# Residual vector quantiser on one core: four shared double PSUM tiles, score tiles of eight groups, another rule for idle products, and a new plan

## The chip, the core and the metric

The kernel runs on one core of a Trainium2 chip. A core has five engines that run side by side, each with an instruction queue of its own: PE (TensorE, matrix products, which write PSUM), DVE (VectorE), ACT (ScalarE), POOL (GpSimd) and SP (SyncE, which here only issues DMAs). PSUM has eight banks; in this kernel a bank holds 512 f32 per partition. The metric is device time in microseconds for one launch; lower is better. One profiled execution, with a trace, stands beside the timed runs.

## What is computed

Input x is (2, 16000, 512) in bf16. A three-tap convolution over time, one weight per tap and channel, is followed by SiLU. Four stages of a residual quantiser follow: in each, the nearest of eight code words is found for every token, subtracted from the residual and added to q. A second three-tap convolution of q gives the output.

```python
for i in range(K):
    z = z + xp[:, i:i+T, :] * dw_enc[i][None, None, :]
z = _silu(z)
for s in range(Nq):                       # Nq = 4, 8 code words each
    d2 = |res|^2 - 2 res.cb + |cb|^2      # (B, T, 8)
    sel = cb[d2.argmin(-1)]
    q = q + sel;  res = res - sel
y = three-tap convolution of q with dw_dec
```

## The kernel before

**Tiling.** The 32,000 tokens form 250 groups of 128, and token p*250+g sits in group g, so the neighbour in time of a token is in the next group at the same place. The groups are worked on in 16 chunks of 12, 14 times 16, and 14 groups (`SIZES`, L26). Channels lie on the 128 partitions in four blocks of 128 (`KT`).

**Front of a chunk** (`front`, L496). SP loads x transposed (L458), up to four groups a DMA. For each channel block DVE makes three tap products (L523). Their two additions run on DVE (L531) or as accumulating DMAs that POOL issues (L529). SiLU is exp, +1, log, exp (ACT L535, DVE L539, ACT L543, L546) and a product on DVE (L551) that writes the residual tile RES. The first chunk is loaded in rows instead (L272, L275), transposed on PE (L427) and copied out of PSUM, blocks 0 and 2 by ACT (L434) and 1 and 3 by DVE (L432).

**A stage** (`stage`, L584). RES holds, beside each 64 tokens, the code words. One product of those 64 tokens with themselves and the code words (L612) therefore gives each token's norm on a diagonal and its products with the eight words. Another product adds a large negative number off the diagonal (L606, `MASK`). DVE takes the maximum of each row, which is the norm (L620), and copies the eight products (L623). A score tile takes up to `GB` = 6 groups, so a chunk of 16 groups has three of 6, 5 and 5. Five small DVE steps (L642 to L666) turn all 16 groups into a one-hot code, PE transposes it (L676), DVE copies it to OHT (L683). In the first three stages RES is then renewed in eight pieces of 1024 elements for two halves of the groups and four channel blocks: either PE forms the selected words (SEL, L700) and DVE adds them (L716), or PE adds words to the old residual (NEW, L721 and L700) and ACT writes it back (L727). After the last stage PE forms the output (Y, L753), ACT copies it (L759) and SP stores it (L763).

**PSUM.** Pool `psG` has two tiles of one bank, for score tiles alone; pool `psA` has three tiles of two banks, for SEL, NEW, Y, the transposed one-hots and the setup (L222, L223).

**Who sets the order.** All steps are tasks of a planner (`Plan`, L55): engine, time held, delay, needs, due time, and the slots that it takes and gives back. A pass puts every task on its engine as soon as engine, needs and slots are free, by rank; passes run forward and backward from ranks with random noise (`ROUNDS`, L47: seed, noise, number of passes). The plan's order is emitted as it stands and every engine runs its own in sequence. A DMA is modelled on one of the servers "SP" (transposing loads), "ACC" (accumulating DMAs) and "OUT" (stores), each with its own line of work.

**Idle products.** Where the plan leaves PE a gap of at least 0.3 us, a psG tile is free and PE was planned busy for less than 60% of the last 4 us, `emit` (L159) puts products into the gap that nobody reads (`warm`, L398; they go to the next score tile, which overwrites them). `ahead` (L409) runs 40 more near the start.

## Time and profile before

| | us |
|---|---|
| three timed runs | 739.68, 749.41, 775.06 (median 749.41) |
| the profiled execution's own time | 744.72 |
| its span, first to last instruction | 742.9 |
| DVE busy in the span | 687.8 |
| ACT busy in the span | 666.7 |
| PE busy in the span | 597.4 |
| mean granted TensorE clock | 0.926 of full speed |

The busy time of an engine counts each moment once. The granted clock is the share of full speed that TensorE was given; a matrix product takes twice as long where it is 0.50. A row such as `L620 DVE TENSOR_REDUCE TR<-PS` names the line of the kernel, the engine, the operation and what is written from what. The duration of one instruction can be longer than the distance to the next one on the same engine, because the next one starts while the last one still ends.

### The profile page before, as it was taken

What the parts mean: (1) busy time and instruction counts of PE and PEld (TensorE: products, weight loads), DVE (VectorE), ACT (ScalarE), POOL (GpSimd) and SP (SyncE); (2) the same over time, 40 slices, a digit from 0 to 9 for tenths busy, and PEclk for the clock granted to TensorE, in tenths of its full rate; (3) what the DMA queues carried; (4) which work ended last, traced back from release to release, by engine and by line L of the source; (5) the groups of instructions that cost most, each with busy time, mean ns of one, the idle gap of its engine ahead of it and who ended that gap; (6) DMA issues with size and microseconds to landing.
All of it is one profiled execution on the core that took longest, in us unless ns stands there. A gap on an engine that the chain in (4) does not pass through costs nothing.

```text
span 742.9 us, 23573 instructions
## 1 busy us (share of the span) xinstructions
PE 597.4 (80%) x10485; PEld 314.9 (42%) x10552; DVE 687.8 (93%) x1359; ACT 666.7 (90%) x539; POOL 78.3 (11%) x104
## 2 busy tenths in 40 slices
PE   4047677898889897888889888988788889889986
PEld 4033334453444344444435443544444443454542
DVE  6999999998999999999999999999999999899942
ACT  2779879998999999999999998989999999975686
POOL 3022100100100011010101001010110001000000
PEclk9558899998998899999999998999999998899999
DMA  7899975979494779668794787979995426220235
GB/s 174 136 188 188 189 136 103 149 137 199 115 209 92 154 175 215 113 175 183 185 210 120 132 164 182 126 210 131 213 185 141 118 58 175 55 88 2 88 142 227
DMA packets 160832, 111.14 MB, mean 150 GB/s; under 512 B 142425, under 2 KB 142810, under 8 KB 160602
## 3 DMA queue, kind: packets, MB, share of 16 engines
q1 hardware_dynamic: 148976, 69.61, 40.2%
q0 software_dynamic: 11472, 39.76, 29.2%
q8 instruction: 82, 1.34, 0.8%
q10 hardware_dynamic: 282, 0.26, 0.1%
q14 instruction: 20, 0.16, 0.1%
HBM read 2.39 MB, written 32.77 MB: 47 GB/s over the span
## 4 chain that ended last, share of the span: by engine, by line
ACT 42%; DVE 28%; PE 17%; issue 5%; DMA 5%; SPq 1%; ACTq 0%; DVEq 0%
ACT RES L727 14%; ACT YSB L759 8%; ACT LN L543 8%; DVE RES L716 8%; ACT E L535 7%; ACT E L546 5%; PE NEW L721 4%; DVE TR L620 3%; PE PS L612 3%; DVE RES L551 3%; PE Y L753 3%; DVE T L523 3%; PE NEW L700 2%; DVE Z L531 2%; DVE E L539 2%
## 5 line engine op out<-in xcount | busy, mean ns | idle before, releaser
L727 ACT ACTIVATE RES<-NEW 128x1024 bf16<-128x1024 f32 (+1 forms) x218 | 219.5, 1052 | 28.4 <-PE NEW L700 21.4
L716 DVE TENSOR_TENSOR RES<-RES,SEL 128x1024 bf16<-128x1024 bf16 (+1 forms) x166 | 196.8, 1197 | 4.1 <-PE SEL L700 3.7
L612 PE MATMUL PS<-RES 128*64 128x80 bf16 (+1 forms) x8064 | 176.4, 203 | 20.7 <-DVE RES L551 18.7
L612 PEld LDWEIGHTS <-RES 128*64 128x64 bf16 x8064 | 172.9, 115 | 28.9 <-DVE RES L551 19.6
L721 PE MATMUL NEW<-RES,IDENT 128*128 128x512 bf16 (+1 forms) x436 | 138.8, 402 | 34.2 <-ACT RES L727 18.0
L759 ACT ACTIVATE YSB<-Y 128x1024 bf16<-128x1024 f32 (+1 forms) x126 | 125.8, 1050 | 17.1 <-PE Y L753 7.4
L535 ACT ACTIVATE E<-Z 128x2048 bf16<-128x2048 bf16 (+1 forms) x64 | 123.0, 1921 | 9.8 <-DVE Z L531 9.7
L543 ACT ACTIVATE LN<-E 128x2048 f32<-128x2048 bf16 (+1 forms) x64 | 123.3, 1927 | 5.9 <-DVE E L539 5.6
L529 POOL DMA_DIRECT2D Z<-T x75 | 69.4, 945 | 543.6 <-issue 77.2
L546 ACT ACTIVATE E<-LN 128x2048 bf16<-128x2048 f32 (+1 forms) x64 | 123.4, 1928 | 0.3
L620 DVE TENSOR_REDUCE TR<-PS 128x5 bf16<-128x320 f32 (+1 forms) x188 | 95.3, 510 | 14.1 <-PE PS L612 13.9
L523 DVE TENSOR_SCALAR T<-XT,WENC 128x2048 bf16<-128x2048 bf16 (+1 forms) x128 | 94.3, 740 | 1.6 <-DMA Z<-T 0.9
L700 PEld LDWEIGHTS <-CBN 32*128 32x128 bf16 x768 | 33.1, 92 | 141.3 <-issue 138.4
L753 PE MATMUL Y<-A,OHT 128*128 128x512 bf16 x214 | 77.3, 388 | 17.6 <-ACT YSB L759 7.2
L700 PE MATMUL NEW<-OHT,CBN 32*128 32x512 bf16 (+1 forms) x436 | 88.1, 400 | 0.0
L700 PE MATMUL SEL<-OHT,CBN 32*128 32x512 bf16 (+1 forms) x332 | 62.0, 399 | 20.2 <-ACT RES L727 9.6
L551 DVE TENSOR_TENSOR RES<-Z,E 128x2048 bf16<-128x2048 bf16 (+1 forms) x64 | 76.9, 1201 | 0.7 <-ACT E L546 0.5
L606 PE MATMUL PS<-MASK,IDENT 128*64 128x320 bf16 (+1 forms) x376 | 64.2, 338 | 4.2 <-DVE PR L623 2.8
L531 DVE TENSOR_TENSOR Z<-Z,T 128x2048 bf16<-128x2048 bf16 (+1 forms) x53 | 62.3, 1177 | 1.9 <-DMA Z<-T 1.8
L721 PEld LDWEIGHTS <-IDENT 128*128 128x128 bf16 x436 | 33.5, 100 | 71.4 <-issue 63.0
L753 PEld LDWEIGHTS <-OHT 128*128 128x128 bf16 x373 | 32.4, 98 | 51.5 <-issue 25.3
L403 PE MATMUL PS<-MASK,IDENT 128*128 128x384 bf16 x175 | 48.8, 373 | 3.1 <-DVE PR L623 2.9
(78 smaller groups left out, 411.8 us busy)
## 6 DMA issues: line engine op xcount, KB each, us to landing
Z<-T POOLq DMA_DIRECT2D x75, 512.0 KB, 5.9
out_dram<-YSB SPq DMA_DIRECT2D x61, 512.0 KB, 3.3
RES<-in_x_dram SPq DMA_DIRECT2D x1, 1664.0 KB, 6.6
XT<-in_x_dram SPq DMA_TRANSPOSE x74, 6.5
out_dram<-YSB SPq DMA_DIRECT2D x1, 384.0 KB, 2.3
out_dram<-YSB SPq DMA_DIRECT2D x1, 256.0 KB, 3.6
A<-in_dw_dec_dram POOLq DMA_DIRECT2D x2, 96.0 KB, 8.0
CB<-in_codebooks_dram ACTq DMA_DIRECT2D x1, 128.0 KB
```

What stands on the lines that cost most here:

```text
L523: nc.vector.tensor_scalar(out=places(u[name]), in0=taps(i, k), scalar1=WENC[:, i, k:k + 1], scalar2=None, op0=ALU.mult)
L535: nc.scalar.activation(u["E"][:, 0:G, :], u["Z"][:, 0:G, :], ACT.Exp, scale=-1.0)
L543: nc.scalar.activation(u["LN"][:, 0:G, :], u["E"][:, 0:G, :], ACT.Ln)
L546: nc.scalar.activation(u["E"][:, 0:G, :], u["LN"][:, 0:G, :], ACT.Exp, scale=-1.0)
L612: nc.tensor.matmul(V[h * HT:(h + 1) * HT, r, :], lhsT=half[:, LC:LC + HT], rhs=half[:, lo:hi], start=False, stop=(i == KT - 1), skip_group ...
L620: nc.vector.tensor_reduce(out=u["TR"][:, q:q + m], in_=u["V", q][:, :, own:own + HT], axis=AX.X, op=ALU.max)
L700: nc.tensor.matmul(ps, lhsT=CBN[s][rows, i * P:(i + 1) * P], rhs=u["OHT"][rows, 0:MB, :], start=start, stop=True, skip_group_check=True)
L716: nc.vector.tensor_tensor(out=old, in0=old, in1=u["SEL", i, j][:, :, 0:W].rearrange("p h (m t) -> p h m t", t=HT), op=ALU.add)
L721: nc.tensor.matmul(NEW[:, h, 0:W], lhsT=IDENT, rhs=tokens(i, j + h, 1), start=True, stop=False, skip_group_check=True)
L727: nc.scalar.activation(old, u["NEW", i, j][:, :, 0:W].rearrange("p h (m t) -> p h m t", t=HT), ACT.Copy)
L753: nc.tensor.matmul(Y[:, h, :], lhsT=lhs(), rhs=rhs, start=(a == 0), stop=(a == len(terms) - 1))
L759: nc.scalar.activation(u["YSB"][:, k:k + n, :], u[k][:, 0:n, :], ACT.Copy)
```

## The change

- Pool psG is gone. psA has four tiles of two banks, and score tiles, SEL, NEW, Y and all others take theirs from it through `bank()`.
- A score tile holds up to eight groups, half of them in each of its two banks: two score tiles instead of three for 16 groups, each with four mask products, one maximum and one copy on DVE.
- An idle product may stand in front of any PE task that takes a psA tile, when one is free in the plan, the gap is at least 0.44 us, and PE was planned busy for less than 75% of the last 3.4 us. It is 512 columns wide instead of 384 and reads the code words instead of the mask. The tile that it wrote goes to the next task that asks for one. The program holds 86 of them (175 before).
- The planner has one server, "DMA", for loads, accumulating DMAs and stores, with new costs; some PE costs are new; noise can be drawn for whole parts of the work (it is set to 0.0 in both rounds); the seeds are new, and with them the order of all tasks.
- The first chunk's rows come in two DMAs instead of one, and the two DMAs for the rows in front of them move from ACT's queue to the front of SP's. PE transposes the first halves of the blocks before the second halves. DVE copies out block 0 alone, ACT blocks 1 to 3. `ahead` needs the identity alone.

In the order of the built programs, DVE does the code words' norms and the code columns of two RES tiles before its first tap product; before the change one RES tile's columns stand there.

```diff
-GB = 6
+GB = 4
-WARM = 0.6
+WARM, WINDOW, TICK = 0.75, 3.4, 0.22
+FIRST_ROWS, ALL_ROWS = 7.8, 10.0
-ROUNDS = [(6060, 1.0, 8), (1653, 1.0, 2)]
+ROUNDS = [(2573, 2.0, 0.0, 8), (7378, 0.3, 0.0, 3)]
...
-                    if free > 0 and sum(b - max(a, end - 4.0) for a, b in spans) < 4.0 * WARM and self.idle():
-                        spans.append((end, end + 0.3))
-                        end += 0.3
-                    else:
-                        end += 0.1
+                    if (free > 0 and "psA" in take and sum(b - max(a, end - WINDOW) for a, b in spans) < WINDOW * WARM
+                            and self.idle()):
+                        spans.append((end, end + TICK))
+                    end += TICK
...
-    psG = ctx.enter_context(tc.tile_pool(name="psG", bufs=2, space=bass.MemoryType.PSUM))
-    psA = ctx.enter_context(tc.tile_pool(name="psA", bufs=3, space=bass.MemoryType.PSUM))
+    psA = ctx.enter_context(tc.tile_pool(name="psA", bufs=4, space=bass.MemoryType.PSUM))
+    pending = []
+    def bank(name):
+        return pending.pop() if pending else psA.tile([P, 2, 512], F32, name=name, tag="psa")
...
-    nc.sync.dma_start(out=XR[:, 1:G + 2, :], in_=xv[:, 0:G + 1, :])
     for b in range(B):
         p = b * HB
-        nc.scalar.dma_start(out=XR[p + 1:p + HB, 0, :], in_=xv[p:p + HB - 1, S - 1, :])
+        nc.sync.dma_start(out=XR[p + 1:p + HB, 0, :], in_=xv[p:p + HB - 1, S - 1, :])
+    HALF = (G + 2) // 2
+    for a, b in ((1, HALF), (HALF, G + 2)):
+        nc.sync.dma_start(out=XR[:, a:b, :], in_=xv[:, a - 1:b - 1, :])
...
-        nc.tensor.matmul(pending[0][:, 0:GB * HT].rearrange("p (r c) -> p r c", c=HT), lhsT=IDENT, rhs=MASK, start=True, stop=True,
-                         skip_group_check=True)
+        nc.tensor.matmul(pending[0][:, 0, :], lhsT=IDENT, rhs=CB4, start=True, stop=True, skip_group_check=True)
...
-            if i % 2:
+            if i == 0:
                 nc.vector.tensor_copy(st["XT"][:, 0:G + 2, i, :], src)
...
-                done.append(plan.add("SP", 0.9 * m, 2.6 + 0.9 * m, [room], due, lambda n=n, m=m: run(n, m)))
+                done.append(plan.add("DMA", 0.7 * m, 2.7 + 0.7 * m, [room], due, lambda n=n, m=m: run(n, m)))
...
-                    return plan.add("ACC", 0.5 + 2.6 * f, 7.0, needs, due, lambda: total(k), give=("T",))
+                    return plan.add("DMA", 0.1 + 2.65 * f, 2.2 + 2.65 * f, needs, due, lambda: total(k), give=("T",))
...
-            PS = pending.pop() if pending else psG.tile([P, 512], F32, name="PS")
-            V = u["V", q] = PS[:, 0:m * (hi - lo)].rearrange("p (r c) -> p r c", r=m)
-            for h in range(2):
-                nc.tensor.matmul(V[h * HT:(h + 1) * HT, :, own:own + HT], lhsT=IDENT[:, h * HT:(h + 1) * HT], rhs=MASK[:, 0:m, :],
-                                 start=True, stop=False, skip_group_check=True)
+            PS = bank("PS")
+            V = u["V", q] = PS[:, :, 0:m // 2 * (hi - lo)].rearrange("p b (r c) -> p b r c", c=hi - lo)
+            for b in range(2):
+                for h in range(2):
+                    nc.tensor.matmul(V[h * HT:(h + 1) * HT, b, :, own:own + HT], lhsT=IDENT[:, h * HT:(h + 1) * HT],
+                                     rhs=MASK[:, 0:m // 2, :], start=True, stop=False, skip_group_check=True)
...
-        banks = -(-G // GB)
+        banks = -(-G // (2 * GB))
...
-            m = -(-(G - q) // (banks - n))
+            m = -(-(G - q) // (2 * (banks - n))) * 2
...
-        plan.add("OUT", 1.5, 3.0, [c], due, store, give=("Y",))
+        plan.add("DMA", 0.6 * len(groups), 0.4 + 0.6 * len(groups), [c], due, store, give=("Y",))
```

## The prediction

> **What bounds the kernel now.** I read the span and busy shares of the page first, then busy time in five stretches (windows), then the waits.

> ```profile
> span 742.9 us, 23573 instructions
> PE 597.4 (80%) x10485; PEld 314.9 (42%) x10552; DVE 687.8 (93%) x1359; ACT 666.7 (90%) x539; POOL 78.3 (11%) x104
> ```

> The columns of the windows are: length; busy us and count of PE, weight load, DVE, ACT, POOL; granted clock; DMA share; GB/s.

> ```profile
> 0.00:20.00 20.00, 8.84 (x104) 8.27 (x104) 13.14 (x41) 5.10 (x4) 6.90 (x25) 0.89 0.84 169
> 20.00:140.00 120.00, 72.18 (x1176) 37.59 (x1177) 115.51 (x212) 102.47 (x72) 18.02 (x17) 0.79 0.89 161
> 140.00:620.00 480.00, 409.92 (x7403) 215.34 (x7455) 467.20 (x913) 466.41 (x379) 50.84 (x60) 0.95 0.75 157
> 620.00:660.00 40.00, 34.07 (x594) 16.90 (x598) 37.35 (x78) 37.05 (x29) 2.57 (x3) 0.87 0.35 94
> 660.00:743.00 83.00, 72.40 (x1212) 36.83 (x1220) 54.63 (x119) 55.67 (x58) 0.00 (x0) 1.00 0.29 116
> ```

> In the long middle, 140 to 620, DVE is idle for 12.8 us and ACT for 13.6: two bounds at once. Work taken from one helps only as far as the other had idle time. From 20 to 140 DVE is the bound (4.5 idle, ACT 17.5). After 660 no engine is full; PE is nearest (10.6 idle), and the last chunks' stages wait for each other.

> Where do the 12.8 and 13.6 us lie? I cut the middle into 80 windows of 6 us. Eleven of them have a granted clock under 0.9. The first, the second and the last of them:

> ```profile
> 140.00:146.00 6.00, 4.76 (x20) 1.44 (x20) 5.93 (x12) 5.79 (x7) 0.00 (x0) 0.72 0.76 111
> ...
> 170.00:176.00 6.00, 5.42 (x21) 1.28 (x19) 5.38 (x9) 3.95 (x4) 0.77 (x1) 0.50 1.05 221
> ...
> 566.00:572.00 6.00, 3.73 (x13) 1.51 (x12) 5.43 (x11) 4.96 (x6) 0.86 (x1) 0.72 0.40 122
> ```

> Summed over the eleven, DVE is idle 7.85 us and ACT 7.83: over half of all idle time in a seventh of the stretch. They are nine episodes (two cover two windows). An episode thus costs 0.87 us on each engine, so between 0.87 (both at once) and 1.74 us of span (one after the other); I take 1.3. Ahead of the one at 170, PE stood still for 1.90 us because its tiles waited for ACT, and then ran at half rate:

> ```profile
> 169.66 0.61 PE L700 MATMUL SEL<-OHT,CBN 32*128 32x512 bf16 x2 [1.90 <-ACT RES L727]
> ```

> **The change part by part.**

> *Score tiles of eight groups.* DVE loses one maximum and one copy of three per stage. The forms, and a stretch that shows distances between starts:

> ```profile
> L620 DVE TENSOR_REDUCE TR<-PS 128x5 bf16<-128x320 f32 x120 | 57.9, 486 | 9.9 <-PE PS L612 9.8
> L620 DVE TENSOR_REDUCE TR<-PS 128x6 bf16<-128x384 f32 x68 | 37.5, 551 | 4.3 <-PE PS L612 4.2
> L623 DVE CAST PR<-PS 128x40 bf16<-128x40 f32 x120 | 22.7, 192 | 0.0
> L623 DVE CAST PR<-PS 128x48 bf16<-128x48 f32 x68 | 13.6, 200 | 0.0
> ```

> ```profile
> 641.59 0.55 DVE L620 TENSOR_REDUCE TR<-PS 128x6 bf16<-128x384 f32 x1
> 642.06 0.68 DVE L539 TENSOR_SCALAR E<-E 128x2048 bf16<-128x2048 bf16 x1
> 642.66 0.20 DVE L623 CAST PR<-PS 128x48 bf16<-128x48 f32 x1
> 642.77 0.48 DVE L620 TENSOR_REDUCE TR<-PS 128x5 bf16<-128x320 f32 x1
> 643.17 1.21 DVE L716 TENSOR_TENSOR RES<-RES,SEL 128x1024 bf16<-128x1024 bf16 x1
> ```

> The next instruction starts 0.47 us after the maximum of six groups, 0.40 after that of five, 0.11 after the copy. So a group adds 0.07 to a maximum, and eight groups should take 0.61; the copy, by 8 ns more from 40 to 48 elements, 0.13. A stage of 16 groups took 0.47+2x0.40+3x0.11 = 1.60 us and will take 2x(0.61+0.13) = 1.48. Saved 0.12 us, in 60 such stages 7 us; the first chunk's four stages have two tiles of six groups before and after. By durations it is more: 2x486+551+2x192+200 = 2107 ns against 2x(681+216) = 1794 (1.0 ns an element onward), 0.31 us a stage, 19 us. The engine is full, so the distance between starts counts: 7 us. Of L620's 95.3 us this lies after 660:

> ```profile
> 660.00:743.00 83.00, 10.65 (x21) 1.00 0.29 116
> ```

> The rest lies where DVE is full, and ACT's 34 idle us before 660 leave room, so I put 6 of the 7 on the path. Bounds: 0 (ACT holds everything) and -19.

> [...]

> PE gets 512 mask products for 376, over the same columns. Their busy time is 39.1 us for 240 of 320 columns and 25.1 for 136 of 384:

> ```profile
> L606 PE MATMUL PS<-MASK,IDENT 128*64 128x320 bf16 x240 | 39.1, 322 | 3.0 <-DVE PR L623 2.1
> L606 PE MATMUL PS<-MASK,IDENT 128*64 128x384 bf16 x136 | 25.1, 365 | 1.2 <-DVE PR L623 0.7
> ```

> That is 163 and 185 ns each, so 141 for 256 columns: 480x0.141+32x0.12 = 71.5, or 7 us more on PE. PE's idle 70 us in the middle hide it; without cover it would cost 7.

> *Four shared tiles.* Nothing shows such a pool. The nearest rows are the waits on either side of psA:

> ```profile
> PE NEW L721 <- ACT RES L727: 18.0, 20, 2.3
> PE SEL L700 <- ACT RES L727: 9.6, 16, 1.9
> ACT RES L727 <- PE NEW L700: 21.4, 28, 2.2
> ```

> ACT waited 21.4 us for NEW in all. A fourth tile lets PE run further ahead; but a score tile now fills one of the four for 64 products, two DVE steps and their place in DVE's queue, and PE's sequence holds SEL, NEW and Y behind a score tile that finds none free. DVE and ACT wait for those. Half of ACT's wait gained is -10, half as much again is +10; the ends are alike, so I take 0.

> *Idle products.* They took PE this long, by stretch:

> ```profile
> 0.00:140.00 140.00, 18.68 (x74) 7.24 (x74) 0.80 0.89 162
> 140.00:620.00 480.00, 24.81 (x85) 7.15 (x85) 0.95 0.75 157
> 620.00:743.00 123.00, 5.29 (x16) 1.36 (x16) 0.96 0.31 109
> ```

> In the changed program's PE order 83 of 86 stand ahead of the end of the second chunk's scores, three in the last chunk, none between. The name says more of them; the middle loses all 85. A product can stand only where a shared tile is free, and the plan's gaps in the middle are not such places. If the episodes do not depend on them: 0, or a little below, for products that held up real work. If each of some forty runs of them had held off an episode: 40x1.3 = +52. The quoted episode came from a wait in which no product stood, which is nearest to the low end; I take +3, two or three episodes more.

> *First rows.*

> ```profile
> 2.06 1.12 ACTq L275 DMA_DIRECT2D RES<-in_x_dram x2
> 9.24 1.65 PE ps_x L427 x14
> 11.14 0.23 DVE L285 TENSOR_SCALAR CBT<-ps_cbt 128x128 bf16<-128x128 bf16 x1 [5.60 <-PE ps_cbt L284]
> 13.91 0.60 DVE L523 TENSOR_SCALAR Z<-XT,WENC 128x1536 bf16<-128x1536 bf16 x1
> 20.80 1.08 DVE L432 COPY XT<-ps_x 128x1792 bf16<-128x1792 bf16 x1
> 23.27 0.62 DVE L300 CUSTOM_DVE_ANT_0 JUNK<-CB 32x512 bf16<-32x512 bf16 x1
> 24.81 0.19 DVE L310 CAST GPOS<-ps_g 128x32 bf16<-128x32 f32 x1 [0.30 <-PE ps_g L309]
> ```

> DVE stands idle for 5.6 us until 11.14 and is full from then on. The norms (23.2 to 25.0, 1.8 us) move into that idle time, and one of two XT copies (1.0) moves to ACT, idle for 15 of the first 20 us. That is -2.8. Against it, the two small DMAs take 1.12 us to issue ahead of the large ones on SP, so the rows, and POOL's copies and the transposing loads that wait for them, may come 1.1 later: between -4 (PE starts with the first half) and +1. I take -3. The code columns only change place, and one more two-element copy on POOL is counted in that 1.1.

> *One DMA server.* The chip's DMA does not change, only the order. What order could win is in the waits for DMA:

> ```profile
> ACT YSB L759 <- DMA out_dram<-YSB: 2.7, 3, 1.9
> DVE Z L531 <- DMA Z<-T: 1.8, 3, 0.8
> ```

> 4.5 us in all, -2 taken; a new order can also cost as much. *Tail.* 13 idle products fewer (0.33 us each, 4.3) against about 1 us of masks, on a PE that is not always the bound: -1 (-4 to +3).

> **Sum.** -6 +0 +3 -3 -2 -1 = -9 on the profiled execution, whose own time is 744.72: 736. The timed median is 749.41, and the four times shown (739.68, 744.72, 749.41, 775.06) have 747.07 as their middle. I predict 747-9 = 738.

> **Rivals.**
> *The clock falls in the middle (slower).* Place: PE between 140 and 620, where no idle product is left. Price 1.3 us an episode. The other terms (-12) are eaten after nine more episodes; 20 above my forecast, one every 16 us in place of one every 53, give 738+26 = 764. For it: over half of today's idle time stands in such windows. Against it: nine came in spite of 85 products, and the quoted one started with tiles full. [...] I give it 0.12.

> *Shared tiles starve ACT.* ACT's 21.4 us for NEW double and DVE's wait goes with it: 738+21 = 759, over the line only with more. For it: a score tile blocks two banks for longer. Against it: two banks that were mostly kept for scores now serve all. 0.05, half of it over the line.

> *The new order wins more.* ACT's idle time from 20 to 140 is 17.5 us, DVE's and ACT's after 660 are 28.4 and 27.3. If the order takes a third off both, -6 and -9 on top: 723. For it: nothing in the early stretch but order holds ACT back while DVE is full. Against it: PE is busy for 72.4 of the last 83 us. 0.38.

> *It does nothing:* ACT holds the middle, the head's gain is lost to the DMAs' issue: 747, within the forecast's case.

> **How the numbers follow.** The forecast's own case, 730 to 750, has 0.45. About 2% is what measuring this kernel can tell from no change: 734.4 and 764.4 here. Faster: 0.38 (the better order, with the low edge of the forecast's case). Slower: 0.12 for the clock, 0.03 for tiles, 0.02 for both in part: 0.17. Same: 0.45. The range goes down to 716 (the better order, with the durations' price for DVE's part) and up to 762 (just under the clock's case): about one in ten left out on either side.

> **What would show it.** 120 maxima near 0.68 us and 120 copies near 0.22; 86 idle products and none from 140 to 620; nine to twelve windows of 6 us under 0.9 (twenty or more: the first rival); ACT's wait for NEW near 21 us; first tap product near 14 with one XT copy on DVE; DVE busy 8 to 20 us less (with the XT copy) and ACT's total 2 more. I am wrong if ACT's idle time in the middle falls below 5 us or passes 25.

## The result, and the profile after

The changed kernel took 799.32 us (median of four runs, 798.2 to 809.2); the kernel before, run beside it, 747.79 (four runs, 739.68 to 775.06). The ratio is 1.0757, 95% interval 1.0619 to 1.0896: slower, outside my range of 716 to 762. The profiled execution took 809.2 us, the slowest of its four; before, 744.72, a little under the median. Executions of one kernel scatter (the kernel before took 739.7 to 776.1 us in its 43 timed runs here, median 758.2), so a profile can lie some 15 us from a typical execution. The head of its page:

```profile
span 807.4 us, 23607 instructions
PE 612.3 (76%) x10599; PEld 325.3 (40%) x10599; DVE 680.9 (84%) x1234; ACT 669.5 (83%) x540; POOL 80.9 (10%) x105
```

DVE has 6.9 us less to do (687.8 before) and ACT 2.8 more, about as planned, but the span is 64.5 us longer. All of it is idle time. Its busy time by stretch (columns as in the prediction):

```profile
0.00:20.00 20.00, 11.21 (x109) 10.37 (x109) 11.90 (x41) 5.20 (x4) 7.24 (x26) 1.00 1.06 197
20.00:140.00 120.00, 69.21 (x919) 34.50 (x921) 100.92 (x175) 92.67 (x68) 15.35 (x14) 0.75 0.86 131
140.00:620.00 480.00, 378.71 (x6645) 196.64 (x6645) 415.86 (x739) 417.93 (x334) 46.98 (x51) 0.85 0.77 145
620.00:660.00 40.00, 31.76 (x595) 16.84 (x590) 36.91 (x64) 36.55 (x30) 6.67 (x9) 0.91 0.85 161
660.00:743.00 83.00, 67.30 (x1393) 38.55 (x1393) 77.18 (x140) 75.77 (x64) 4.65 (x6) 0.98 0.34 91
743.00:807.40 64.40, 54.09 (x951) 28.37 (x951) 38.13 (x79) 41.38 (x44) 0.00 (x0) 0.96 0.31 124
```

DVE's idle time rose from 6.9 to 8.1 us in the first 20 us, from 4.5 to 19.1 up to 140, from 12.8 to 64.1 in the middle, and from 31.0 to 35.2 behind 620: 71.4 in all, less 6.9 of work gives the 64.5. In the middle DVE, ACT and PE are all further from full than before, so no engine's work is the bound there; they wait. For what, the waits say (engine, tile and line waited for: us in total, times, longest):

```profile
DVE TR L634 <- PE PS L626: 55.4, 33, 6.2
DVE Z L543 <- DMA Z<-T: 16.1, 5, 8.2
DVE RES L730 <- PE SEL L714: 14.0, 12, 7.7
...
DVE T L535 <- DMA Z<-T: 7.6, 4, 3.6
```

DVE's wait for scores was 13.9 (9.8 and 4.2 in the two forms shown in the prediction), for accumulating DMAs 3 or less, for SEL 3.7. ACT's wait for NEW went from 21.4 to 38.3:

```profile
ACT RES L741 <- PE NEW L714: 38.3, 37, 5.1
```

PE is waited for, and yet it is busy for only 76%. Part of the answer is a stop that the kernel before does not have. A piece of the timeline (start, duration, instruction; in brackets the idle time in front of it and what released it):

```profile
377.31 14.17 SPq L468 DMA_TRANSPOSE XT<-in_x_dram  x1
...
385.01 0.30 DVE L662 TENSOR_TENSOR KEY<-V,GPOS 128x128 bf16<-128x128 bf16 x1
...
390.49 0.61 PE L768 MATMUL Y<-A,OHT 128*128 128x512 bf16 x1 [9.35 <-issue]
...
391.14 1.02 ACT L774 ACTIVATE YSB<-Y 128x1024 bf16<-128x1024 f32 x1 [8.75 <-PE Y L768]
...
392.96 1.22 DVE L730 TENSOR_TENSOR RES<-RES,SEL 128x1024 bf16<-128x1024 bf16 x1 [7.65 <-PE SEL L714]
```

PE stands still for 9.35 us in front of a product of Y, with no tile, engine or DMA named as its releaser ("issue"); DVE and ACT then wait for PE. The same happens ten times behind 50 us, for 1.7 to 9.4 us, 38.5 in all; before, no such stop reaches 1 us. What they have in common is a count. Windows from 0 to just ahead of the first, the sixth and the tenth of them, at 120.57, 390.49 and 666.54:

```profile
0.00:120.55 120.55, 64.64 (x863) 37.81 (x863) 94.95 (x182) 85.67 (x61) 19.78 (x38) 0.78 0.96 148
...
0.00:390.45 390.45, 275.25 (x4447) 146.44 (x4447) 324.19 (x594) 308.76 (x237) 46.13 (x66) 0.81 0.82 139
0.00:666.50 666.50, 495.16 (x8415) 261.83 (x8415) 571.90 (x1030) 558.86 (x438) 76.58 (x100) 0.84 0.79 144
```

Products and weight loads add up to 1726, 8894 and 16830. The differences, 7168 and 7936, are 28 and 31 times 256; divided by 256, each count leaves 190, as at all ten stops. I call the places in PE's order with this remainder edges, and the 256 products and weight loads between two of them a block. And the DMA queues in the window of the long stop (381 to 390.5; packets, MB, share of the 16 engines' time):

```profile
q1 hardware_dynamic: 1067, 0.56, 84.3%
q0 software_dynamic: 83, 0.29, 22.0%
q8 instruction: 1, 0.02, 1.9%
```

One packet of the "instruction" kind lies in it, while the data queues keep the DMA engines full at 91 GB/s. Its record begins at 386.27 and takes 2.93 us; PE goes on 1.29 us behind its end. At all ten stops PE goes on 1.29 to 1.49 us behind the end of such a packet. At the other edges behind 50 us the packet had ended at least 1.3 us ahead, and no stop is longer than 0.23 us. There is one packet of queue q8 for 256 products and weight loads of PE (before: 82.2 times 256, after: 82.8, and the kernel e15 below, which has more of them: 106.2):

```profile
q8 instruction: 82, 1.34, 0.8%
```

```profile
q8 instruction: 83, 1.36, 0.7%
```

```profile
q8 instruction: 106, 1.74, 0.9%
```

I read a stop as PE waiting for a block of instructions that such a packet brings; the trace itself names no releaser. Counted from the edge before, the packet has ended after 2.1 us in the median; at the ten stops it took 2.9 to 12.0, and PE had started the 256 instructions in between within 2.3 to 4.2 us. So all ten have both, a block used up fast and a packet that ends late. The share of the DMA engines during the stops is 1.02 to 1.28 at nine of them and 0.00 at the tenth (664.46 to 666.53).

### The profile page after: what moved, and what is told of

Same layout as the page of the kernel before. It is cut to its first block, busy times and chain, and to the rows that moved or that the text cites. A ratio compares the mean times of both kernels' runs of the same rounds, so it can differ in the third digit from the quotient of the medians.

```text
span 807.4 us, 23607 instructions
## 1 busy us (share of the span) xinstructions
PE 612.3 (76%) x10599; PEld 325.3 (40%) x10599; DVE 680.9 (84%) x1234; ACT 669.5 (83%) x540; POOL 80.9 (10%) x105
## 3 DMA queue, kind: packets, MB, share of 16 engines
q8 instruction: 83, 1.36, 0.7%
## 5 line engine op out<-in xcount | busy, mean ns | idle before, releaser
L741 ACT ACTIVATE RES<-NEW 128x1024 bf16<-128x1024 f32 (+1 forms) x215 | 213.9, 1032 | 47.6 <-PE NEW L714 38.3
L626 PE MATMUL PS<-RES 128*64 128x72 bf16 (+1 forms) x8064 | 180.0, 208 | 56.3 <-issue 29.4
L626 PEld LDWEIGHTS <-RES 128*64 128x64 bf16 x8064 | 177.0, 120 | 59.6 <-issue 30.7
L735 PE MATMUL NEW<-RES,IDENT 128*128 128x512 bf16 (+1 forms) x430 | 149.8, 435 | 45.0 <-ACT RES L741 21.0
L774 ACT ACTIVATE YSB<-Y 128x1024 bf16<-128x1024 f32 (+1 forms) x124 | 123.2, 1037 | 27.5 <-PE Y L768 22.2
L547 ACT ACTIVATE E<-Z 128x2048 bf16<-128x2048 bf16 (+1 forms) x64 | 121.9, 1909 | 24.7 <-DVE Z L543 15.7
L555 ACT ACTIVATE LN<-E 128x2048 f32<-128x2048 bf16 (+1 forms) x64 | 122.0, 1905 | 17.7 <-DVE E L551 17.5
L634 DVE TENSOR_REDUCE TR<-PS 128x8 bf16<-128x512 f32 (+1 forms) x128 | 87.0, 682 | 55.6 <-PE PS L626 55.4
L768 PE MATMUL Y<-A,OHT 128*128 128x512 bf16 x245 | 89.4, 417 | 23.3 <-issue 9.3
L714 PE MATMUL NEW<-OHT,CBN 32*128 32x512 bf16 (+1 forms) x430 | 94.5, 436 | 0.2
L714 PE MATMUL SEL<-OHT,CBN 32*128 32x512 bf16 (+1 forms) x330 | 60.2, 410 | 29.5 <-ACT RES L741 10.5
L620 PE MATMUL PS<-MASK,IDENT 128*64 128x256 bf16 (+1 forms) x512 | 55.8, 300 | 8.9 <-DVE RES L730 4.4
L768 PE MATMUL Y<-B,OHT 128*128 128x512 bf16 x122 | 51.1, 418 | 0.0
## 6 DMA issues: line engine op xcount, KB each, us to landing
A<-in_dw_dec_dram POOLq DMA_DIRECT2D x2, 96.0 KB, 10.9
```

What stands on the lines that cost most here:

```text
L547: nc.scalar.activation(u["E"][:, 0:G, :], u["Z"][:, 0:G, :], ACT.Exp, scale=-1.0)
L555: nc.scalar.activation(u["LN"][:, 0:G, :], u["E"][:, 0:G, :], ACT.Ln)
L626: nc.tensor.matmul(V[h * HT:(h + 1) * HT, r // (m // 2), r % (m // 2), :], lhsT=half[:, LC:LC + HT], rhs=half[:, lo:hi], start=False, stop ...
L634: nc.vector.tensor_reduce(out=u["TR"][:, q:q + m].rearrange("p (b r) -> p b r", b=2), in_=u["V", q][:, :, :, own:own + HT], axis=AX.X, op= ...
L714: nc.tensor.matmul(ps, lhsT=CBN[s][rows, i * P:(i + 1) * P], rhs=u["OHT"][rows, 0:MB, :], start=start, stop=True, skip_group_check=True)
L735: nc.tensor.matmul(NEW[:, h, 0:W], lhsT=IDENT, rhs=tokens(i, j + h, 1), start=True, stop=False, skip_group_check=True)
```

## The experiments

Every kernel keeps the change's or the old kernel's code but for the lines shown or the parts named. Times are medians; "stops" are PE's stops of 1 us or more for "issue" behind 50 us. The table puts all runs side by side; idle is DVE's, in us. The start column has the time of the first tap product and the chunk that it belongs to (its tiles are 1536 wide in the first chunk, 2048 in the second). The kernel before gave 761.2, 761.9, 751.1, 758.6 and 766.2 beside the five sets of runs.

| run | us | start | idle 0-40 | 40-140 | 140-620 | stops: n, us |
|---|---|---|---|---|---|---|
| before | 747.8 | 13.9, first | 7.3 | 4.1 | 12.8 | 0 |
| after | 799.3 | 18.4, first | 8.1 | 19.1 | 64.1 | 10, 38.5 |
| e1 before, no idle products | 763.5 | 13.4, first | 6.8 | 5.7 | 28.3 | 0 |
| e9 before, more idle products | 755.2 | 13.2, first | 6.8 | 4.2 | 12.1 | 1, 1.1 |
| e3 before, small additions | 748.5 | 12.8, first | 6.4 | 5.1 | 16.6 | 0 |
| e2 after, small additions | 754.8 | 17.9, first | 7.5 | 7.7 | 24.6 | 5, 9.2 |
| e5 before, after's seeds | 780.7 | 23.2, second | 17.4 | 9.8 | 25.2 | 0 |
| e12 before, third seed | 772.4 | 14.3, first | 7.6 | 11.0 | 27.2 | 0 |
| e14 before, new first rows | 793.2 | 35.9, second | 26.0 | 10.6 | 25.1 | 1, 1.4 |
| e6 before, one server | 792.7 | 13.3, first | 6.6 | 32.5 | 28.6 | 1, 2.2 |
| e8 before, new tiles | 772.1 | 14.5, first | 8.8 | 11.4 | 35.5 | 5, 11.9 |
| e16 new tiles, after's seeds | 791.7 | 20.1, second | 16.3 | 14.1 | 34.7 | 6, 17.3 |
| e7 after, three servers | 800.0 | 34.1, second | 24.5 | 10.6 | 38.3 | 2, 5.9 |
| e10 after, old landing times | 811.8 | 23.6, second | 19.1 | 18.9 | 38.5 | 4, 6.3 |
| e13 after, third seeds | 826.4 | 27.2, second | 22.1 | 15.7 | 60.2 | 9, 16.9 |
| e17 after, loads held back | 801.6 | 18.2, first | 7.8 | 13.5 | 55.5 | 8, 19.0 |
| e4 after, before's seeds | 848.3 | 35.2, second | 25.5 | 25.0 | 88.3 | 5, 12.6 |
| e11 after, six groups | 845.4 | 35.2, second | 25.7 | 14.1 | 69.0 | 3, 9.1 |
| e15 before, split products | 787.8 | 13.9, first | 7.3 | 12.2 | 38.3 | 4, 9.4 |
| e18 before, early loads | 757.0 | 14.9, first | 8.1 | 10.3 | 14.4 | 1, 1.6 |

The profiled executions of e4 and e11 took 861.4 and 848.2 us, more than the medians here, so their idle times are high ends.

**The clock, first rival.** The mark that I had set for it is there: of the 80 windows of 6 us in the middle, 35 have a granted clock under 0.9 (11 before). What a clock of 0.50 does to a product, the trace of before shows: two products of NEW (L721) in a row start 0.400 us apart (median of 18 pairs) for 0.225 at 1.00 (192 pairs), and one lasts 0.61 us for 0.38, less than twice as long. To see what the windows cost, I took the idle products away, in the same order of all other work (e1: `WARM = 0.6` to `0.0`), and doubled them (e9, with this edit: 357 instead of 175).

```diff
-WARM = 0.6
+WARM = 0.85
...
-                    if free > 0 and sum(b - max(a, end - 4.0) for a, b in spans) < 4.0 * WARM and self.idle():
+                    if free > 0 and sum(b - max(a, end - 3.4) for a, b in spans) < 3.4 * WARM and self.idle():
```

> The kernel before, its plan and order unchanged, with none of its 175 idle products between the others (the 40 at the start stay). Theory C (the clock): the changed kernel is slow because its middle has no idle products and PE falls to half rate; then this kernel shows most of that loss too, 780 us or more, with 25 or more windows of 6 us under 0.9 of the clock between 140 and 620. Theory D (DMA jams): the loss comes from DMAs that run into each other and hold up data and PE's instructions; then this kernel stays within 745 to 765, with 12 to 18 such windows, and no stop of PE for 'issue' longer than 2 us.

> The kernel before, its order unchanged, with 357 idle products instead of 175 (threshold 85% of the last 3.4 us instead of 60% of 4). Theory C': half-rate windows cost the span what my forecast said, 1.3 us an episode; then the windows of 6 us under 0.9 between 140 and 620 fall from 11 to 5 or fewer, DVE's and ACT's idle time there from 13 to 8 us or less, and the time is 5 to 10 us under the kernel before of this call. If idle products hold up real work as much as they save: within 5 us, or slower.

Without any, 28 windows are under 0.9 and the time is 763.5 against 761.2 beside it: 2 us, or 17 against the fastest run of that set (746.7), either way of a size with the scatter. With twice as many, seven windows, clock 0.98, ratio 0.9974 (0.9905 to 1.0043). Rows of the middle, e1 and e9:

```profile
140.00:620.00 480.00, 400.33 (x7144) 209.54 (x7143) 451.68 (x881) 452.21 (x365) 49.13 (x57) 0.89 0.79 155
```

```profile
140.00:620.00 480.00, 425.59 (x7570) 221.87 (x7569) 467.87 (x915) 466.79 (x379) 51.60 (x60) 0.98 0.79 158
```

The rival's mark came, and as the main cause the rival is refuted: 28 slow windows, without one stop of PE, cost 2 to 17 us and not 52. A small share is not excluded. In the old order the missing idle products alone bring 28 windows; how many of the 35 follow PE's stops is not shown.

**The load of the accumulating DMAs.** Both kernels with the same order, but each accumulating DMA adds one group of 16 (32 KB for 512); the other groups' additions are left out of the computation.

```diff
-                    nc.gpsimd.dma_start(out=z, in_=t, accum_op=ALU.add)
+                    nc.gpsimd.dma_start(out=z[:, 0:1, :], in_=t[:, 0:1, :], accum_op=ALU.add)
```

> The changed kernel with its order unchanged, but each accumulating DMA adds one group of the 16 (so the additions of the other groups are left out). Theory D: with a sixteenth of these DMAs' bytes the jams go, and with them PE's stops for 'issue' (10 of 1.5 us or more after 100 us) and the waits for DMA; time 725 to 765. Theory C: PE's gaps stay, 785 or more. Theory T (the four shared tiles starve ACT and DVE): 785 or more, with ACT's and DVE's waits for PE as they were.

> The kernel before with the same cut: each accumulating DMA adds one group of the 16. Its waits for DMA are under 5 us, so by theory D little is to be won, 730 to 748; by theories C and T the same. It is the control for the small adds in the changed kernel.

After falls from 799.3 to 754.8. Before gives 748.5, with 761.2 for the full kernel beside it. Of DVE's waits in e2, those for accumulating DMAs are gone, and PE's stops are 9.2 us for 38.5:

```profile
DVE TR L634 <- PE PS L626: 38.5, 37, 3.7
DVE OHT L697 <- PE ps_oh L690: 5.1, 8, 1.5
```

With small additions the two are 6 us apart, with full ones 52. So some 45 of the 52 us need these additions in full: in the old order they cost at most 13 us by these medians, in the new one they are waited for. Beside waits by DVE and ACT that name a DMA (36.5 us in after, 6.1 before), PE's stops are longer with them: in e2 every packet of instructions has ended 3.9 us behind the edge before it at the latest, in after 12.0. Which share belongs to the bytes and which to the sooner landing of a small addition this pair does not tell.

**Order or rules?** The seeds, with their noise and passes, crossed (e4: after with before's, e5: before with after's), and a third draw of each (e12, e13).

```diff
-ROUNDS = [(6060, 1.0, 8), (1653, 1.0, 2)]
+ROUNDS = [(2573, 2.0, 8), (7378, 0.3, 3)]
```

> The changed kernel with the seeds, noise and passes of the kernel before (6060 with 1.0 and 8 passes, 1653 with 1.0 and 2), so another draw of the order under the same rules. Theory S (an unlucky draw): 770 or less. Theories C, D with the one server as the cause, and T (something that every draw has): 785 to 820.

> The kernel before with the changed kernel's seeds, noise and passes alone (2573 with 2.0 and 8, 7378 with 0.3 and 3): another order under the old rules. Theory S (the old order was an unusually good draw and any other loses): 775 or more, with waits for DMA over 15 us. Otherwise 740 to 765.

> The kernel before with another first seed (303 instead of 6060), all else as it was. Theory S (the old order is an unusually good draw): 768 or more. If the draw matters little: 745 to 765.

> The changed kernel with another pair of seeds (101 and 202), everything else as it is. If the changed kernel's 50 us come from an unlucky order that its seeds drew, another order of the same rules is near the kernel before: 745 to 765. If they come from the rules (one DMA server with short landing times, score tiles of eight groups), they come back with any order: 780 to 850, with 40 or more slices of 1 us in which the DMA engines are full and move under 120 GB/s (19 before, 49 in the changed kernel), and stops of PE for its own instructions.

Some expectations count slices of 1 us in which DMA engines are at least 0.9 full and move under 120 GB/s. They are 19 in before, 49 in after, but 26 in e13, 21 in e7, 23 in e10, and 30 in e17, which has after's order: the count is no measure of the loss.

Both order and rules matter. The old rules gave 748 to 766, 781 and 772 (e12: 1.0305, 1.0214 to 1.0396): the old order was a good draw, and each of two others costs some 20 us. The new rules gave 799, 848 and 826 (e13: 1.0911, 1.0717 to 1.1106). The table says where. The middle's idle time is 12.8, 25.2, 27.2 under the old rules and 64.1, 60.2 (and 88.3) under the new: two groups, whatever the seeds. (e1 and e9 share the order of before and have 28.3 and 12.1. How much of that is scatter and how much the idle products is not shown, so I call differences under some 16 us in this column no finding.) The start changes with the draw: where the order lets DVE begin with the second chunk, 16 to 26 us of the first 40 are idle instead of 6 to 9. In e14, e7, e4 and e11 DVE waits 17 to 19 us of this for the second chunk's transposed loads; in e5, e16, e10 and e13 the profile names no releaser for 5 to 10 us. In e14:

```profile
35.88 0.75 DVE L528 TENSOR_SCALAR Z<-XT,WENC 128x2048 bf16<-128x2048 bf16 x1 [18.45 <-DMA XT<-in_x_dram]
```

The changed kernel's own order begins with the first chunk and does not have that loss. But of the seven orders drawn with the new first rows six begin with the second chunk, of the six with the old first rows two: the change may favour that start, which so few draws do not show.

**The parts.** One server alone in the old kernel (e6: the four lines of the diff with `"DMA"`, of which one is shown); three servers in the new one (e7: the four old lines); the new lines, but with the old, longer times to landing (e10); the new tiles, groups and idle rule alone in the old kernel, with its seeds (e8) and with the new ones (e16); the new kernel with six groups to a tile (e11: `GB = 3`, a third seed).

```diff
-                    return plan.add("ACC", 0.5 + 2.6 * f, 7.0, needs, due, lambda: total(k), give=("T",))
+                    return plan.add("DMA", 0.1 + 2.65 * f, 2.2 + 2.65 * f, needs, due, lambda: total(k), give=("T",))
```

> The kernel before with the one DMA server and its costs alone, old seeds. Theory D1 (the server's order lets DMAs collide): 785 or more, with jams (microseconds with the DMA engines over 0.9 busy and under 120 GB/s) well over 19 and waits for DMA over 20 us. Theory T1 (jams hurt only with the shared tiles of eight groups): 740 to 765. A theory that the one server helps: under 740.

> The changed kernel with the three DMA servers and costs of the kernel before, the rest as changed. Theory D1: back to 765 or less, jams under 30. Theory T1: 785 or more, PE's stops for 'issue' still there.

> The changed kernel, one DMA server, but with the landing times of the kernel before in the plan (accumulating DMA 7.0 us after its start instead of 4.85, a load of four groups 6.2 instead of 5.5, a store 3.0 instead of 2.8). Theory L (the plan promises data before the chip has it): DVE's and ACT's waits for DMA fall from 32 us to 12 or less and the time to 785 or less. If the shared server itself is at fault: waits for DMA stay over 20 us, 790 or more.

> The kernel before with the four shared double tiles, score tiles of eight groups and the new idle products alone (old servers, PE costs, seeds and first rows). Theory T1: 785 or more, with stops of PE for 'issue' over 1 us. Theory D1: 740 to 765, none or few such stops. Had the tiles alone been what I forecast (-6 for DVE, +3 for the clock): 735 to 750.

> The four shared tiles with score tiles of eight groups and the rule for idle products, on the old servers, costs and first rows, with the seeds of the changed kernel: the same part as the run that gave 772, in another order. If the tiles cost by themselves, it stays near 770 to 800, with stops of PE for its own instructions again. If 772 was an unlucky order, it may be 740 to 760. The old rules with these seeds gave 781.

> The changed kernel with the four shared tiles, but score tiles of up to six groups (6, 6 and 4), seeds 303 with noise 1.0 and then as changed (with the changed kernel's seeds the plan finds no end). Theory F (PE's instruction blocks): runs of 256 PE instructions in under 4 us fall from 27 to 12 or fewer, and stops of PE for 'issue' of 1 us or more from 10 to 2 or fewer. If the stops come from DMA jams alone: 5 or more. Time 765 to 800, since the order is drawn anew.

By times alone e7 and e10 would say that the server is harmless: 800 and 812. But both drew a start with the second chunk, which takes 16 and 11 us more than after's. Their middle, three servers first, then old landing times:

```profile
140.00:620.00 480.00, 399.82 (x7150) 214.37 (x7148) 441.68 (x791) 443.35 (x357) 53.44 (x57) 0.87 0.77 154
```

```profile
140.00:620.00 480.00, 391.03 (x7003) 207.59 (x6999) 441.51 (x783) 436.19 (x354) 49.43 (x56) 0.88 0.75 151
```

DVE's idle time there is 38.3 and 38.5, against 64.1 in after and 55.5 in e17, which has after's order: with the old landing times, on one server or on three, 17 to 26 us of the middle come back. DVE's waits in the middle alone say which (140 to 620; after, then e7):

```profile
DVE TR L634 <- PE PS L626: 27.7, 17, 4.5
DVE Z L543 <- DMA Z<-T: 13.9, 3, 8.2
...
DVE T L535 <- DMA Z<-T: 4.0, 3, 3.3
```

```profile
DVE TR L634 <- PE PS L626: 24.9, 20, 4.1
...
DVE T L535 <- DMA Z<-T: 3.6, 2, 3.1
```

The wait for accumulating DMAs falls from 17.9 to 3.6 (1.1 in e10); the wait for scores stays. Over all draws with full additions DVE waits 13.5 to 58.8 us for DMAs in the middle with the new landing times and the new tiles, and 0.4 to 13.1 with the old times: the groups all but touch, so one draw alone would not tell. The planned 2.2+2.65 = 4.85 us from an accumulating DMA's start to its landing is what the new order counts on, where the old one counts on 7.0; the trace shows 5.9 as the median from issue to landing in both kernels, and up to 17.7 in the new one (10.7 before). In the old kernel the one server (e6) costs as well: DVE waits 37.8 us for DMAs (3.3 before), mostly ahead of 140; being one draw, it is no price.

The tiles: against the old rules with the same seeds +10 and +11 us at least (772 for 761.9 beside it, 792 for 781), and 35.5 and 34.7 idle in the middle, above all three draws of the old rules, though within the scatter of the highest. Stops of 11.9 and 17.3 us appear, which those draws do not have. And the maxima's wait for scores in the middle is 14 to 33 us in every run with eight groups to a tile, 20 in e11, and 4 to 10 in every run with the old tiles but e15. The stops are only part of this: in e7 they make 5.9 us in all, and the wait is 24.9. e11 does not clear the tiles' share: its stops are 9.1 us, but its DMA waits are high (60.0 for DVE), and its start is the second chunk's.

**PE's stops.** Do stops come where PE goes through 256 instructions fast? In the old kernel, same order, each product of a stage's first score tile is issued as two, 40 columns and the rest: about 3000 more products and weight loads.

```diff
-                        nc.tensor.matmul(V[h * HT:(h + 1) * HT, r, :], lhsT=half[:, LC:LC + HT], rhs=half[:, lo:hi],
-                                         start=False, stop=(i == KT - 1), skip_group_check=True)
+                        for a, b in ((0, 40), (40, hi - lo)) if q == 0 else ((0, hi - lo),):
+                            nc.tensor.matmul(V[h * HT:(h + 1) * HT, r, a:b], lhsT=half[:, LC:LC + HT], rhs=half[:, lo + a:lo + b],
+                                             start=False, stop=(i == KT - 1), skip_group_check=True)
```

> The kernel before, same order of tasks, with each score product of a stage's first score tile issued as two (the first 40 columns, then the rest): nothing else changes, but PE gets 3000 products and 3000 weight loads more, close together. If PE stops where 256 instructions have been used up faster than the next 256 come, stops of PE with no releaser over 1 us appear here too (none before), at counts of PE instructions that agree modulo 256, and runs of 256 instructions under 4 us rise from 5 to 15 or more; the time rises by these stops and by some of 3000 x 0.01 to 0.02 us of PE: 755 to 790. If the stops belong to the shared tiles or to the new order, there are none.

Four stops, 9.4 us, inside the split products. The longest, and the counts ahead of the first and of this one:

```profile
183.13 2.43 PE L613 MATMUL PS<-RES 128*64 128x40 bf16 x89 [4.29 <-issue]
```

```profile
0.00:102.80 102.80, 48.91 (x735) 29.76 (x735) 83.92 (x162) 68.45 (x46) 20.39 (x37) 0.70 0.90 162
0.00:183.10 183.10, 111.90 (x2141) 66.05 (x2143) 153.65 (x301) 133.95 (x96) 27.28 (x45) 0.80 0.84 142
```

1470 and 4284 leave 190 and 188: the same edge, in a kernel with the old tiles and the old order (2141 products stand beside 2143 weight loads; with the two records that this lacks, 190 again). Stretches of 256 PE instructions that start within 4 us, taken from the trace one behind the other without overlap, rose from 17 to 54; the changed kernel has 46, all others with the old tiles have 9 to 16 (the expectations' 5 and 27 are counted in another way). So the split products alone brought stops to the old order, 9.4 us where before has none. A tile of eight groups asks PE for 64 pairs of weight load and product and four masks in one go, over half a block. It is not the only source: in e11, with six groups but all the rest new, there are 32 such stretches and the stops make 9.1. Time 787.8, ratio 1.0427 (1.0244 to 1.061), of which the stops are 9.4; PE's added work is in it too.

**The start.** The first rows alone in the old kernel (e14) drew an order that starts with the second chunk, so its 35.9 us answer another question; its last rows landed at 10.9. In the changed kernel the first two transposing loads of the second chunk stand on SP without the wait for POOL's copies, which the old order has; e17 restores it, e18 takes it from the old kernel.

```diff
+            nc.gpsimd.memset(st["XT"][0:1, 0:G + 2, 0, 0:2], 0.0)
```

> The kernel before with the change of the first rows alone (two loads on SP behind the two small ones, first halves of the blocks transposed first, three copies on ACT and one on DVE). The planner draws another order, so the time says little (745 to 785 by the other draws). The start says it: if the new first rows are what delays the first tap product, it begins near 18 us, as in the changed kernel, and PE's transposes near 11.8. If the delay is the order's, it begins near 14 or sooner.

> The changed kernel with one more write of POOL (36 elements, behind its copies for the first rows) that touches every group of the second chunk's tile of x, so that all its transposing loads wait for the first rows and the code words; in the changed kernel the first two of them stand on SP with no such wait. Order as it is. If these two loads delay the start: second half of the rows there by 7.5 to 8.5 (9.87 in the changed kernel), code words by 8.6 (10.3), first tap product at 14 to 15 us (18.96), and the time 3 to 6 us less, 793 to 797. If the rows' own split and place on SP delay it, the first tap product stays at 17 to 19 us and the time at 799. How late the second chunk's x then lands is the risk: its loads begin 6 us later.

> The kernel before with POOL's four small copies put into another group of the second chunk's tile of x, one that the third load on SP fills: the first two transposing loads no longer wait for the first rows and run beside them, as in the changed kernel. Order as it is. If that is what delays the start: first rows landed at 9 to 10 us (7.4), first tap product at 17 to 19 (13.9), time 3 to 8 us more than before. If not, the first tap product stays near 14 us and the time within 1%.

The theory fell: the first tap product comes at 18.23 us in e17 (18.43 in after) and at 14.89 in e18 (13.91). The early loads are worth 0.2 to 1.0 us. The rest is in the rows and in PE's order, which no run here separates. When the last rows are there, POOL's copy shows: 7.44 us before, 9.87 in after, 9.50 in e17 (one fence for each):

```profile
7.44 0.18 POOL L475 COPY XT<-RES 1x2 bf16<-1x2 bf16 x1 [5.91 <-DMA RES<-in_x_dram]
```

```profile
9.87 0.17 POOL L486 COPY XT<-RES 1x2 bf16<-1x2 bf16 x1 [3.76 <-DMA RES<-in_x_dram]
...
10.34 0.68 DVE L309 CUSTOM_DVE_ANT_0 JUNK<-CB 32x512 bf16<-32x512 bf16 x1 [3.78 <-DMA CB<-in_codebooks_dram]
...
11.69 0.18 PE L318 MATMUL ps_g<-DIAG,ONES 32*128 32x32 bf16 x1 [5.46 <-DVE DIAG L316]
11.80 1.68 PE L435 MATMUL ps_x<-IDENT,RES 128*128 128x128 bf16 x14
```

```profile
9.50 0.17 POOL L486 COPY XT<-RES 1x2 bf16<-1x2 bf16 x1 [2.56 <-DMA RES<-in_x_dram]
...
10.02 0.68 DVE L309 CUSTOM_DVE_ANT_0 JUNK<-CB 32x512 bf16<-32x512 bf16 x1 [3.46 <-DMA CB<-in_codebooks_dram]
```

PE's first transposes, at 9.24 before, start at 11.80, behind the norms' product ps_g, which waits for DVE's norms and so for the code words; the first half of the rows had been there since 5.94. e17's four runs took 793 to 815 us (after 798 to 809), so its time is not told apart from that of after. Its profiled execution, of 793.3 us, has 19.0 us of stops, after's, of 809.2, has 38.5: the same order stops for different times in different executions.

## Why the prediction was wrong

**DVE's work, -6: the size held, its worth did not.** The maximum of eight groups took 690 ns where I had worked out 681, and the copy 221 (216):

```profile
L634 DVE TENSOR_REDUCE TR<-PS 128x8 bf16<-128x512 f32 x120 | 82.5, 690 | 48.8 <-PE PS L626 48.5
L637 DVE CAST PR<-PS 128x64 bf16<-128x64 f32 x120 | 25.5, 221 | 0.0
```

DVE's busy time fell by 6.9 us, of which about 1 is the XT copy that went to ACT: some 6 for the scores where I had 7, and under the 8 to 20 that I had set as a mark. But I put 6 on the path because DVE was full; with 64 us idle in the middle, it is not, and the gain went into waiting.

**Four shared tiles, 0 (±10): value and mechanism failed.** The part costs 10 us or more in two draws. I had looked at tiles held and at ACT's wait for NEW; that wait is 18.5 and 23.5 in e8 and e16 (21.4 before), so tiles do not starve ACT. What I had not priced is PE's stops at the edges of 256 (11.9 us in e8, 17.3 in e16; e15 has 9.4 with the old tiles), and DVE's wait for scores, 16.3 and 14.2 in the middle of e8 and e16 (5.2 and 9.5 with the same seeds and the old tiles). How tiles and stops share that wait is not shown.

**One DMA server, -2: the step that failed most.** I took what order could win from the waits for DMA, 4.5 us, and wrote that a new order can cost "as much". That is no bound on a loss: the small waits were a property of the one order that had been drawn. With the new landing times DVE and ACT wait 36.5 us for DMAs, and the middle is idle for 17 to 26 us more than with the old ones (e7, e10). Both parts are smaller with small additions (e2: 9.2 us of stops for 38.5, and 4.1 us of waits by DVE and ACT that name a DMA for 36.5), so their prices do not simply add up to the 64 us of the middle. By my own sign of error, ACT's idle time in the middle above 25 us, the forecast had failed: it is 62.1.

**Idle products and clock, +3: not contradicted, but the price was wrong.** 1.3 us an episode was idle time that stood beside an episode. e1 puts all of them together at 2 to 17 us, where forty episodes would have been 52, and e9 finds nothing to win.

**First rows, -3: the gain did not come.** The first tap product comes 4.5 us later. That is not 4.5 us lost, since DVE now does the norms and a second tile's code columns ahead of it; but its idle time in the first 20 us rose by 1.2 us, where I had the norms fill 1.8 us of it. I charged 1.1 us for the small loads' issue, and the rows came 2.1 to 2.4 later; and I let the norms move into idle time without seeing that PE has ps_g ahead of the transposes in its order.

**The rival "the new order wins more", 0.38, had the wrong sign.** I counted idle time that an order could fill, not what it could open. The order before was the fastest of all drawn here.

**The tail, -1,** was not tried alone: DVE's idle time behind 620 rose by 4.2 us with everything changed.

**Open.** How much of the 64 us in the middle falls to PE's stops, how much to waits for data, and what else makes DVE wait for scores where stops are few (e7, e10). That the stops end with a late block of instructions is my reading of the packets' ends, the count and the rate; no run moved these packets alone. No kernel here beats the kernel before; e9 equals it.

## What to carry to other kernels

Where a planner draws the order, the waits in the profile are those of one draw: before you credit a new plan, redraw the old one with two other seeds, and read start and middle apart, since one may hide what the other shows. Hold a model's landing times against the traced ones: with 4.85 us planned for an accumulating DMA, where the trace has a median of 5.9, DVE waited 17.9 us for them in the middle, with 7.0 planned 3.6 and 1.1 (e7, e10), and no busy share foretold it. A mark set for a rival proves nothing until the mark is changed alone: the slow windows came (28 in e1), and cost 2 to 17 us.
